# Turning the exponentials through DRAM and VectorE, and making the right sides' sums a batch earlier, in an attention and MLP kernel bound by TensorE

## The chip, the cores and the metric

One core of a Trainium2 chip runs the whole kernel. The metric is device microseconds of one execution. Each kernel below was executed several times; medians and ranges are given. A run whose granted TensorE clock fell far below 1 is called slow and is left out of every comparison.

## The reference, cut to what matters

```python
B, H, S, Ns, D = 8, 8, 512, 32, 64            # x: (B,H,S,D), state: (B,H,Ns,D)
a     = softmax(scale * x @ state.T)          # tokens read the state
xread = a @ state
a2    = softmax(scale * state @ x.T)          # the state reads the tokens
sread = a2 @ x
t     = concat(xread, sread) -> (B * 544, 512)
out   = gelu_quick(t @ w_in) @ w_out          # 512 -> 2048 -> 512, all in float32
```

A "batch" below is one of the 8 values of B: 512 tokens that pass through both matrices.

## The kernel before

The down product of a batch (2048 to 512) is made by Strassen's scheme with seven products P1 to P7 of blocks. Some of the seven are themselves made by a second level, again seven products of 128-column blocks: "two-level". While TensorE works on batch b, VectorE and ACT prepare batch b + 1 through hooks, which are called between the products by name: "P6.3" is after the third small product of P6. A small product is eight matmuls, and below it is called an "eight". T1 to T4 are sums of blocks of `w_out`, the right sides of P5, P6, P7 and P4; P3 has the block B22. In the hooks, `x_scale` and `x_back` are steps of the tokens' side of the attention (division, transposes back); `att_eT` and `eT_turn` belong to the state's side.

For sread, the exponentials of the scores `e` (state rows by tokens) must be turned so that tokens are rows. TensorE did it, between P6 and P3 of the batch before:

```python
def att_eT(b, g):
    ps = att_ps([P, SCH, P], f"eT_{b}_{g}")
    for c in range(SCH):
        nc.tensor.transpose(ps[:, c], a["e2"][g][0][:, P*c : P*(c+1)], ident)
    nc.scalar.copy(a["eT"][:, g], ps)
...
def s_norm(b, g):                              # e is divided by its sum, on ACT
    nc.scalar.activation(out=e, in_=e, func=AF.Copy, scale=sm)
```

Batch 1 was `plain`: only P6 and P7 of it were two-level, since the sums of the right sides (blocks of `w_out`) for the second level were only made on VectorE during batch 1:

```python
if plain:
    p5 = bank(0)
    product(p5, [S1[:, f, :half] for f in range(HF)], T1, "P5")
...
ahead = {   # VectorE's work for later batches, hung into batch 1
    "P1a": low_sums(T2, low_a) + [(low_keep, ...), (T_of, (T4, B21, T2)), (low_third, (T2,))],
    "P1b": low_sums(T3, low_b) + [(low_keep, ...), (low_third, (T3,))],
    "P4.7": low_sums(T1, low_b) + [...],
}
for k, step in zip((4, 5, 6), low_sums(B22, low_a)):
    ahead[f"P7.{k}"] = [step]
```

A set of sums (three 128x512 pieces, 768 KB) is kept in DRAM and reloaded before its product; there is SBUF room for two sets, and one more for T4's.

```python
def low_load(k, i):
    nc.sync.dma_start(turn_rooms[i], outside[k])
```

## Time and profile before

| | before |
|---|---|
| time, median (range) | 718.16 us (718.05 to 718.18, 4 runs) |
| span of the profiled run | 716.2 us |
| TensorE busy / VectorE busy | 703.9 us (98%) / 586.9 us (82%) |
| start of the next batch's scores to the same in the next batch, batches 2 to 6 | 76.43 us |
| the same in batch 1 | 79.19 us |

The last two rows are the useful clock of this kernel. In TensorE's timeline each batch has one row of scores (output `o`, input `xsq`), and the distance of these rows is the length of a batch. The prediction shows the lines of the profile. In a timeline the columns are start, duration, engine, line, instruction, tiles and shapes, how many were merged and, in brackets, how long the engine idled before and what ended that. Of the tiles, `eT` holds the turned exponentials, `sr` is the result of the state read (sread), and `M` is what the states give with `w_in`.

### The profile page before, as it was taken

The page shows a single profiled execution, that of the slowest core. Times are in us where ns is not written, and L with a number is a line of the kernel's source. Part 1 is how long each engine was busy: PE and PEld are TensorE (multiplying, and loading weights), DVE is VectorE, ACT ScalarE, POOL GpSimd, SP SyncE. Part 2 cuts the span into 40 slices and gives each one's busy share as a digit, 9 for nine tenths or more (in the row PEclk, how much of TensorE's full clock was granted, in tenths as well). Part 3 has the DMA queues.
Part 4 walks back from the last instruction along what each step waited for, and adds up shares of the span by engine and source line. Part 5 has one row for each costly group of instructions (what it writes and reads, how often), then busy time and mean ns, then how long its engine had stood idle before and what let it go on. Part 6 is the DMA issues. An engine that isn't in the chain of part 4 may idle for free.

```text
span 716.2 us, 12329 instructions
## 1 busy us (share of the span) xinstructions
PE 703.9 (98%) x4949; PEld 561.0 (78%) x4951; DVE 586.9 (82%) x1199; ACT 241.8 (34%) x467; POOL 0.8 (0%) x8
## 2 busy tenths in 40 slices
PE   8989999999999999999999999999999999999996
PEld 3433444457898799889998899879987998899995
DVE  6999899739968998789878997898779987888650
ACT  5686511024214331424233422442243324300210
POOL 0000000000000000000000000000000000000000
PEclk9999999999999999999999999999999999999999
DMA  8921246016145234405450444132431440022001
GB/s 228 364 83 58 97 148 130 24 59 152 56 166 73 47 117 162 78 1 118 138 144 3 83 168 125 28 74 94 174 62 29 133 148 30 1 70 108 17 1 29
DMA packets 104362, 68.43 MB, mean 96 GB/s; under 512 B 87665, under 2 KB 95345, under 8 KB 104305
## 3 DMA queue, kind: packets, MB, share of 16 engines
q1 hardware_dynamic: 104304, 67.65, 33.4%
q8 instruction: 39, 0.64, 0.4%
q14 instruction: 19, 0.15, 0.1%
HBM read 54.79 MB, written 12.85 MB: 94 GB/s over the span
## 4 chain that ended last, share of the span: by engine, by line
PE 90%; DVE 3%; DMA 2%; ACT 2%; issue 0%; SPq 0%; DVEq 0%; ACTq 0%
PE low L669 19%; PE o L1071 17%; PE o L720 14%; PE o L669 9%; PE o L518 7%; PE h L500 7%; PE upx L1071 6%; PE M L320 4%; PE o L561 2%; PE o L320 1%; PE sr L480 1%; PE warm L125 1%; PE upx_sr L1071 1%; DMA out_dram<-osb_sr 1%; PE eT L469 1%; DMA out_dram<-osb 1%
## 5 line engine op out<-in xcount | busy, mean ns | idle before, releaser
L1081 DVE TENSOR_TENSOR g<-o,g 128x512 f32<-128x512 f32 (+1 forms) x140 | 88.0, 650 | 51.5 <-PE o L1071 50.5
L720 PE MATMUL o<-w_out,g 128*128 128x256 f32 x480 | 107.9, 381 | 0.0
L720 PEld LDWEIGHTS o<-w_out,g 128*128 128x128 f32 x480 | 90.1, 190 | 18.4 <-issue 6.3
L1078 ACT ACTIVATE g<-g 128x512 f32<-128x512 f32 (+1 forms) x84 | 49.8, 600 | 100.8 <-DVE g L1081 100.8
L1071 PE MATMUL upx<-aT,M 128*128 128x256 f32 x192 | 49.3, 379 | 0.0
L1071 PE MATMUL o<-ta,M 128*128 128x256 f32 x192 | 49.3, 379 | 0.0
L1071 PE MATMUL o<-ta,ms 128*128 128x256 f32 x192 | 48.3, 379 | 0.0
L460 ACT COPY M<-M 128x512 f32<-128x512 f32 x64 | 33.2, 596 | 29.7 <-PE M L320 29.7
L1071 PEld LDWEIGHTS o<-ta,ms 128*128 128x128 f32 x192 | 36.5, 190 | 5.0
L1071 PEld LDWEIGHTS o<-ta,M 128*128 128x128 f32 x192 | 36.5, 190 | 5.0
L669 PE MATMUL low<-low,g 128*128 128x128 f32 x304 | 40.2, 275 | 0.0
L1071 PEld LDWEIGHTS upx<-aT,M 128*128 128x128 f32 x192 | 36.1, 190 | 4.7
L669 PEld LDWEIGHTS low<-low,g 128*128 128x128 f32 x304 | 37.0, 192 | 0.0
L669 PE MATMUL low<-sums,later 128*128 128x128 f32 x264 | 35.0, 276 | 0.1
L669 PEld LDWEIGHTS low<-sums,later 128*128 128x128 f32 x264 | 32.7, 192 | 0.7 <-DVE pu L674 0.3
L320 PE MATMUL M<-w_in,stT 64*32 64x512 f32 x512 | 32.7, 594 | 0.2 <-ACT eT L470 0.2
L541 DVE TENSOR_TENSOR later<-g,g 128x512 f32<-128x512 f32 (+1 forms) x32 | 20.8, 649 | 14.3 <-ACT g L503 14.3
L500 PE MATMUL h<-low,M 128*128 128x512 f32 x64 | 29.7, 600 | 1.5 <-DVE low L408 1.5
L500 PE MATMUL h<-aT,M 128*128 128x512 f32 x64 | 28.7, 599 | 1.4 <-ACT M L460 1.4
L518 PE MATMUL o<-w_out,g 128*128 128x512 f32 x64 | 28.7, 594 | 0.0
L669 PE MATMUL low<-w_out,g 128*128 128x128 f32 x216 | 28.5, 275 | 0.0
L518 PE MATMUL o<-w_out,sums 128*128 128x512 f32 x64 | 28.4, 594 | 0.0
(214 smaller groups left out, 1287.9 us busy)
## 6 DMA issues: line engine op xcount, KB each, us to landing
low<-low SPq DMA_DIRECT2D x34, 768.0 KB
later<-in_moe_w_out_dram SPq DMA_DIRECT2D x16, 512.0 KB
xn<-in_x_dram SPq DMA_DIRECT2D x28, 256.0 KB
w_out<-in_moe_w_in_dram SPq DMA_DIRECT2D x12, 512.0 KB
xsq<-in_x_dram SPq DMA_DIRECT2D x96, 64.0 KB
out_dram<-osb SPq DMA_DIRECT2D x18, 256.0 KB
out_dram<-later SPq DMA_DIRECT2D x14, 256.0 KB
later<-in_moe_w_in_dram SPq DMA_DIRECT2D x4, 512.0 KB
```

The source lines that it names most:

```text
L125: nc.tensor.matmul(ps, zeros[:, :P], zeros, start=True, stop=True)
L320: nc.tensor.matmul(ps[g][st], A[b]["stT"][rows, st], rhs(rows, j), start=True, stop=True)
L460: nc.scalar.copy(m[:, g], ps[g])
L500: nc.tensor.matmul(hps, lhs[i], rhs[i], start=(i == 0), stop=(i == n - 1))
L518: nc.tensor.matmul(ops, G[key, f // 2][:, f % 2, P * r : P * (r + 1)], w_out[:, f], start=(f == 0), stop=(f == NF - 1))
L541: nc.vector.tensor_tensor(out=s1, in0=a21, in1=a22, op=ALU.add)
L561: nc.tensor.matmul(ps[:, r], lhs[f][:, P * r : P * (r + 1)], rhs[:, f], start=(first and r == 0 and f == 0), stop=(f == HF - 1), skip_grou ...
L669: nc.tensor.matmul(ps, lhs[f], rhs[:, f], start=(first and f == 0), stop=(f == QF - 1), skip_group_check=True)
L720: nc.tensor.matmul(ps[:, r], lhs[f][:, P * r : P * (r + 1)], rhs[:, f], start=(r == 0 and f == 0), stop=(f == HF - 1), skip_group_check=True,)
L1071: nc.tensor.matmul(ps[:, k], lhs[i][:, o : o + P], rhs[i], start=(first and k == 0 and i == 0), stop=(i == n - 1), skip_group_check=True,)
L1078: nc.scalar.activation(out=dst, in_=src, func=AF.Gelu_apprx_sigmoid)
L1081: nc.vector.tensor_tensor(out=dst, in0=ps, in1=x, op=ALU.add)
```

## The change

Its intent: take work off the engine that is the bound. The turns leave TensorE: `e` goes to DRAM in runs of 128 B, comes back with its 32x32 blocks in the right places, and VectorE turns each block. The division by the sums moves behind the state read. A reload is cut into three, in the order in which its parts are read. VectorE's sums for P6, P5, P3 and P7 are made in a hole, a stretch in which VectorE idles, at the end of batch 0, so that P5, P3 and P4 of batch 1 become two-level too. The core of the diff:

```diff
+    def eT_out(b):
+        for j in range(NPR):
+            src = e2_room[b][Ns*j : Ns*(j+1), :NG].rearrange("n g (t a) -> n (g t) a", a=Ns)
+            nc.sync.dma_start(squares[:, :, j], src)
+    def eT_in(b):
+        v = squares.rearrange("n (k i) j a -> i n k (j a)", i=SCH)
+        for i in range(SCH):
+            nc.sync.dma_start(a["eT"][Ns*i : Ns*(i+1)].rearrange("n g c q -> n (g c) q"), v[i])
+    def eT_turn(b, g):
+        t = A[b]["eT"][:, g].rearrange("p c q -> p (c q)")
+        nc.vector.transpose(t, t)
...
     def low_load(k, i):
-        nc.sync.dma_start(turn_rooms[i], outside[k])
+        for n in (1, 0, 2):
+            nc.sync.dma_start(low[:, 3*i + n], outside[k][:, FC*n : FC*(n+1)])
...  (hooks of the next batch)
-            ("P6.4", x_scale, 0), ("P6", att_eT, 0), ("P6", att_eT, 1),
-            ("P3.3", x_scale, 1), ("P3.4", x_back, 0), ("P3.5", x_back, 1)
+            ("P6.6", x_scale, 1), ("P3.3", x_back, 0), ("P3.4", x_back, 1),
+            ("P3.5", eT_turn, 0), ("P3.6", eT_turn, 1), ("P5", eT_in),
...  (end of batch 0)
         if f == NF - 2:
             T_of(T1, B12, B11)
+            low_away(6, B22)
+            low_made(5, T1, 1)
...
             T_of(B12, B22, B12)
+            low_away(3, T3)
+            low_third(T3)
             turn_x(2)
+            low_made(2, T2, 0)
...  (batch 1: all `plain` branches are gone)
+    ahead = {"P1a": [(low_third, (B22,)), (T_of, (T4, B21, T2)), (low_third, (T2,))],
+             "P7.7": [(low_third, (T4,))]}
```

More of the change, by code (lines that the diff above doesn't have):

```diff
@@ L360, in att_s_max @@
             a["mx2"].append(mx)
+    e2_room = {}
     def att_s_exp(b, room=None):
@@ L364, in att_s_exp @@
         if room is None:
-            room = apool.tile([P, NPR, S], FP32, tag="xT", name=f"e2_{b}")
+            room = e2_room[b] = apool.tile([P, NPR, S], FP32, tag="xT", name=f"e2_{b}")
         a["e2"] = []
@@ L379, in s_norm @@
             nc.vector.tensor_scalar(e, e, sm, None, ALU.mult)
-        else:
-            nc.scalar.activation(out=e, in_=e, func=AF.Copy, scale=sm)
     def att_s_norm(b):
@@ L460, in att_M @@
             nc.scalar.copy(m[:, g], ps[g])
+    squares = dram.tile([Ns, NG * NB, NPR, Ns], FP32, name="squares")
+    def eT_out(b):
+        for j in range(NPR):
+            src = e2_room[b][Ns * j : Ns * (j + 1), :NG].rearrange("n g (t a) -> n (g t) a", a=Ns)
+            nc.sync.dma_start(squares[:, :, j], src)
+    def eT_in(b):
+        a = A[b]
+        a["eT"] = apool.tile([P, NG, SCH, P], FP32, tag="eT", name=f"eT_{b}")
+        v = squares.rearrange("n (k i) j a -> i n k (j a)", i=SCH)
+        for i in range(SCH):
+            nc.sync.dma_start(a["eT"][Ns * i : Ns * (i + 1)].rearrange("n g c q -> n (g c) q"), v[i])
+    def eT_turn(b, g):
+        t = A[b]["eT"][:, g].rearrange("p c q -> p (c q)")
+        nc.vector.transpose(t, t)
     def att_eT(b, g):
@@ L484, in att_sread @@
         sr = apool.tile([P, P], FP32, tag="sr", name=f"sr_{b}")
-        nc.scalar.copy(sr, ps.rearrange("p g d -> p (g d)"))
+        if b < 2:
+            nc.scalar.copy(sr, ps.rearrange("p g d -> p (g d)"))
+        else:
+            for g in range(NG):
+                nc.scalar.activation(out=sr[:, D * g : D * (g + 1)], in_=ps[:, g], func=AF.Copy, scale=a["e2"][g][1])
         A[b]["sr"] = sr
@@ L618, in low_load @@
     def low_load(k, i):
-        nc.sync.dma_start(turn_rooms[i], outside[k])
+        for n in (1, 0, 2):
+            nc.sync.dma_start(low[:, 3 * i + n], outside[k][:, FC * n : FC * (n + 1)])
     def low_keep(k, src):
@@ L635, in low4_make @@
         low_keep(4, t)
+        a["low4"] = t
     def low4_load(a):
@@ L699, in strassen_two @@
     def strassen_two(key, dst, hooks, a4):
-        plain = a4 is None
         B11, B21, B22 = w_out[:, :HF, :HN], w_out[:, HF:, :HN], w_out[:, HF:, HN:]
@@ L767, in strassen_two @@
         nc.scalar.copy(k1, bank(0))
-        if plain:
-            sums_of((S2, (q1, q2, q4)))
-        else:
-            *r, p5 = spare_M()
-            r = [v.rearrange("p (k h t) -> p k h t", k=2, h=2) for v in r]
-            p5 = p5.rearrange("p (r n) -> p r n", r=2)
-            sums_of((S1, r), (S2, (q1, q2, q4)))
-            third_of(S1)
+        *r, p5 = spare_M()
+        r = [v.rearrange("p (k h t) -> p k h t", k=2, h=2) for v in r]
+        p5 = p5.rearrange("p (r n) -> p r n", r=2)
+        sums_of((S1, r), (S2, (q1, q2, q4)))
+        third_of(S1)
         product(bank(1), A_of(0, 1), B21, "P2")
@@ L787, in strassen_two, with at @@
         o, h0, h1 = low_banks()
-        if plain:
-            for fn in first:
-                fn()
-            p5 = bank(0)
-            product(p5, [S1[:, f, :half] for f in range(HF)], T1, "P5")
-            banks = [h0, h1, o]
-        else:
-            def at(i):
-                for fn in first[i - 1 : i]:
-                    fn()
-                hook(f"P5.{i}")
-            b11, t3, b21, b22 = halves_of(T1)
-            strassen_low(left_of(S1, *r), (b11, t3, b21, b22, *low_b), [h0, h1, o], p5, at)
-            low_load(6, 1)
-            o, h0, h1 = low_banks()
-            banks = [h0, o, h1]
+        def at(i):
+            for fn in first[i - 1 : i]:
+                fn()
+            hook(f"P5.{i}")
+        b11, t3, b21, b22 = halves_of(T1)
+        strassen_low(left_of(S1, *r), (b11, t3, b21, b22, *low_b), [h0, h1, o], p5, at)
+        low_load(6, 1)
+        hook("P5")
+        o, h0, h1 = low_banks()
+        banks = [h0, o, h1]
         def sums(y, rooms):
@@ L842, in strassen_two @@
         steps4, left4 = sums(y_of(NU, half), (q1, q2, q4))
-        own6 = {}
-        if not plain:
-            steps12, left12 = sums(y_of(NU, 0), r)
-            own6 = {2: steps12[:1], 5: steps12[1:2]}
+        steps12, left12 = sums(y_of(NU, 0), r)
+        own6 = {2: steps12[:1], 5: steps12[1:2]}
         lowly("P6", left_of(S2, q1, q2, q4), T2, low_a, banks, k2, own6)
-        if not plain:
-            low_load(3, 0)
+        low_load(3, 0)
         tt(k2, k2, k1)
         tt(t01, p5, k2)
-        if plain:
+        hook("P6")
+        p3 = o01
+        o, h0, h1 = low_banks()
+        own3 = {1: steps12[2:3], 2: steps12[3:]}
+        if key + 1 == B:
+            own3.update({i + 3: steps3[i : i + 1] for i in range(4)})
+        lowly("P3", left12, B22, low_b, [h0, h1, o], p3, own3)
+        if key + 1 < B:
+            low_load(5, 1)
+        hook("run")
+        if key + 1 < B:
             for fn in steps3:
                 fn()
-            hook("P6")
-            p3 = bank(3)
-            product(p3, A_of(0, 1), B22, "P3")
-            o, h0, h1 = low_banks()
-            lowly("P7", left3, T3, low_b, [h0, h1, o], k3, {})
-        else:
-            hook("P6")
-            p3 = o01
-            o, h0, h1 = low_banks()
-            own3 = {1: steps12[2:3], 2: steps12[3:]}
-            if key + 1 == B:
-                own3.update({i + 3: steps3[i : i + 1] for i in range(4)})
-            lowly("P3", left12, B22, low_b, [h0, h1, o], p3, own3)
-            if key + 1 < B:
-                low_load(5, 1)
-            hook("run")
-            if key + 1 < B:
-                for fn in steps3:
-                    fn()
-            hook("T")
-            o, h0, h1 = low_banks()
-            lowly("P7", left3, T3, low_a, [o, h0, h1], k3, {k + 1: steps4[k : k + 1] for k in range(4)})
-            if key + 1 < B:
-                low_load(2, 0)
+        hook("T")
+        o, h0, h1 = low_banks()
+        lowly("P7", left3, T3, low_a, [o, h0, h1], k3, {k + 1: steps4[k : k + 1] for k in range(4)})
+        if key + 1 < B:
+            low_load(2, 0)
         osb = opool.tile([P, 2, HN], FP32, tag="osb", name=f"osb_{key}_11")
@@ L887, in strassen_two @@
         ]
-        if not plain:
-            o, h0, h1 = low_banks()
-            lowly(
-                "P4", left4, T4, low_parts(a4["low4"]), [o, h1, h0], k1, {2: then[:2], 3: then[2:3], 4: then[3:]}
-            )
-            p4 = k1
-        else:
-            for fn in then:
-                fn()
-            product(bank(2), A_of(1, 1), T4, "P4")
-            for i in range(1, 8):
-                hook(f"P4.{i}")
-            p4 = bank(2)
+        o, h0, h1 = low_banks()
+        lowly(
+            "P4", left4, T4, low_parts(a4["low4"]), [o, h1, h0], k1, {2: then[:2], 3: then[2:3], 4: then[3:]}
+        )
+        p4 = k1
         tt(o10, p4, k3)
@@ L920, in hooks_next @@
         at("P2a", att_s_exp, b)
+        at("P2a", eT_out, b)
         at("P2a", x_max, b, 0)
         at("P2a", x_sub, b, 0)
-        if b > 2:
-            at("P5.1", x_exp, b, 0)
-            at("P5.6", att_s_norm, b)
-            at("P5.6", x_max, b, 1)
-            at("P5.7", x_sub, b, 1)
-            at("P6.1", x_exp, b, 1)
-        else:
-            at("P2a", x_max, b, 1)
-            at("P2a", x_sub, b, 1)
-            at("P2a", x_exp, b)
-            at("P2", att_s_norm, b)
+        at("P5.1", x_exp, b, 0)
+        at("P5.6", att_s_norm, b)
+        at("P5.6", x_max, b, 1)
+        at("P5.7", x_sub, b, 1)
+        at("P6.1", x_exp, b, 1)
         steps = up_sums(b)
@@ L937, in hooks_next @@
         attention = [
-            ("P6.1", x_sum, 0), ("P6.3", x_sum, 1), ("P6.3", x_inverse), ("P6.4", x_scale, 0), ("P6", att_eT, 0), ("P6", att_eT, 1),
+            ("P6.1", x_sum, 0), ("P6.3", x_sum, 1), ("P6.3", x_inverse), ("P6.4", x_scale, 0),
         ]
-        if b > 2:
-            attention += [("P3.3", x_scale, 1), ("P3.4", x_back, 0), ("P3.5", x_back, 1)]
-            names = {"T": range(5), "P7.5": (5, 6), "P7.6": (7,), "P4.1": (8,), "P4.5": (12, 13)}
-            run, turned = "run", "P7.2"
-        else:
-            attention += [("P6.5", x_scale, 1), ("P6.6", x_back, 0), ("P6", x_back, 1)]
-            names = {"P3a": range(7), "P7.1": (7,), "P7.2": (8,), "P7.3": (12, 13)}
-            run, turned = "P3a", "P3b"
-        attention += [(run, att_sread), (run, att_M, 3, True), (run, att_M, 2)]
+        attention += [
+            ("P6.6", x_scale, 1), ("P3.3", x_back, 0), ("P3.4", x_back, 1), ("P3.5", eT_turn, 0), ("P3.6", eT_turn, 1),
+            ("P5", eT_in), ("run", att_sread), ("run", att_M, 3, True), ("run", att_M, 2),
+        ]
+        names = {"T": range(5), "P7.5": (5, 6), "P7.6": (7,), "P4.1": (8,), "P4.5": (12, 13)}
         for name, fn, *args in attention:
@@ L953, in hooks_next @@
                 at(name, steps[i][0], *steps[i][1])
-        at(turned, att_srT, b)
+        at("P7.2", att_srT, b)
         return h
@@ L1223, in T_of, with low_made, low_away @@
         nc.vector.tensor_tensor(out=t, in0=x0, in1=x1, op=ALU.subtract)
+    def low_made(k, t, i):
+        for fn, args in low_sums(t, (low_a, low_b)[i]):
+            fn(*args)
+        low_keep(k, turn_rooms[i])
+    def low_away(k, t):
+        room = apool.tile([P, NPR, S], FP32, tag="xT", name=f"away_{k}").rearrange("p j t -> p (j t)")[:, : 3 * FC]
+        for fn, args in low_sums(t, low_parts(room)):
+            fn(*args)
+        low_keep(k, room)
     rest = list(range(2 * nper, NF))
@@ L1250 @@
             T_of(T2, B22, T1)
+            low_third(T1)
         if f == NF - 1:
@@ L1264 @@
             ahead = {"P1a": [(up_strassen(b, S, *parts_x(b), A[b]["sums"]), ())]}
-            if b == 2:
-                ahead["P3.6"] = [(low_third, (T4,))]
-        else:
-            ahead = {
-                "P1a": low_sums(T2, low_a)
-                + [(low_keep, (2, turn_rooms[0])), (T_of, (T4, B21, T2)), (low_third, (T2,))],
-                "P1b": low_sums(T3, low_b) + [(low_keep, (3, turn_rooms[1])), (low_third, (T3,))],
-                "P4.7": low_sums(T1, low_b) + [(low_keep, (5, turn_rooms[1])), (low_third, (T1,)), (low_third, (B22,))],
-            }
-            for k, step in zip((4, 5, 6), low_sums(B22, low_a)):
-                ahead[f"P7.{k}"] = [step]
-            ahead["P7.6"] += [(low_keep, (6, turn_rooms[0])), (low_load, (2, 0))]
+        else:
+            ahead = {"P1a": [(low_third, (B22,)), (T_of, (T4, B21, T2)), (low_third, (T2,))], "P7.7": [(low_third, (T4,))]}
         if b + 1 < B:
@@ L1293 @@
         a4 = {}
-        at = hooks.setdefault("run" if b > 1 else "P3a", [])
+        at = hooks.setdefault("run", [])
         k = 3 if b + 1 < B else 0
         at[k:k] = [(low4_load if b > 1 else low4_make, (a4,))]
-        strassen_two(b, out_of(b), hooks, a4 if b > 1 else None)
+        strassen_two(b, out_of(b), hooks, a4)
         if b + 2 < B:
```

## The prediction

> **What bounds the kernel now.** I read the busy shares first, then the chain that ended last, then one table of windows by stage, and then the timelines of TensorE and VectorE inside two batches. From the page, the busy shares and the chain's share by engine:
>
> ```profile
> PE 703.9 (98%) x4949; PEld 561.0 (78%) x4951; DVE 586.9 (82%) x1199; ACT 241.8 (34%) x467; POOL 0.8 (0%) x8
> ...
> PE 90%; DVE 3%; DMA 2%; ACT 2%; issue 0%; SPq 0%; DVEq 0%; ACTq 0%
> ```
>
> TensorE is busy for 98% and carries 90% of the chain. The ends of matmuls are modelled, so I check with starts. In the windows (length, then PE, PEld, DVE and ACT busy with counts), batch 1 is the first row and two later batches follow:
>
> ```profile
> 154.30:233.50 79.20, 78.89 (x539) 67.22 (x538) 61.69 (x112) 25.56 (x47) 0.00 (x0) 1.00 0.43 111
> 233.50:310.00 76.50, 76.50 (x612) 68.08 (x611) 66.40 (x140) 27.26 (x54) 0.00 (x0) 1.00 0.35 94
> 310.00:386.50 76.50, 76.50 (x612) 68.08 (x611) 65.80 (x139) 27.26 (x54) 0.00 (x0) 1.00 0.36 95
> ```
>
> From batch 2 on TensorE never stops. The scores of the next batch start at 244.53, 320.96, 397.39, 473.82 and 550.25 us in the chain: a period of 76.43 us each time, so a later batch is worth exactly its TensorE instructions. Batch 1 runs from 165.27 to 244.53, 79.26 us, which is 2.83 more. Part of that is its three plain products, part is waiting. VectorE has about 10 us free in 76.5, but not evenly. Around P3 of the batch at 386 us (start, duration, instruction, in brackets the idle time before it):
>
> ```profile
> 416.37 0.29 DVE L674 TENSOR_TENSOR later<-o,pu 128x128 f32<-128x128 f32 x1 [0.48 <-PE o L669]
> ...
> 419.10 0.29 DVE L674 TENSOR_TENSOR pu<-low,pu 128x128 f32<-128x128 f32 x1 [0.24 <-PE low L669]
> ...
> 420.81 0.29 DVE L674 TENSOR_TENSOR later<-o,pu 128x128 f32<-128x128 f32 x1 [0.16 <-PE o L669]
> ...
> 423.49 0.29 DVE L674 TENSOR_TENSOR later<-low,pu 128x128 f32<-128x128 f32 x1 [0.60 <-PE low L669]
> ```
>
> There are 1.48 us of slack in these 7 us; from 391 to 415 us it has hardly any.
>
> **What the Trainium skill says.** "VectorE: DVE Perf Modes", section "The three transpose paths": TensorE turns a whole 128x128 into PSUM, VectorE only 32x32 blocks. That is why the new route needs a trip through DRAM to place the blocks besides VectorE's turn. The trace has the sizes for fp32: TensorE 8 instructions (two 128x512 turns) in 0.89 us, VectorE 0.68 us for each 128x512. "DMA: Bandwidth & Descriptors", section "Specifications": below 512 B a transfer is not at line rate. The new trip writes runs of 32 floats, 128 B. The trace agrees on the kind: the squares of x, also 128 B runs, 1 MB, take about 10 us (440.7 to 452 in the DMA row, 105 to 145 GB/s), while the 768 KB reloads reach 415 GB/s. Its section "Two DMAs through the same engine are not ordered": a DMA that reads what another wrote must wait for the completion semaphore; here that is a wait on the queue's issuing engine, which holds back what stands behind it. The kernel before has such pairs (sums kept in DRAM and reloaded), but tens of microseconds apart, so its trace doesn't time this wait.
>
> **The change part by part.**
>
> 1. Transposes of the exponentials off TensorE. Timeline of TensorE, the two-level product before, the transposes and the product after:
>
> ```profile
> 415.27 1.06 PE L669 MATMUL o<-low,later 128*128 128x128 f32 x8
> 416.17 1.04 PE L469 MATMUL eT<-ident,e 128*128 128x128 f32 x8
> 417.04 1.06 PE L669 MATMUL low<-w_out,g 128*128 128x128 f32 x8
> ```
>
> From 416.17 to 417.04 is 0.87 us; the general spacing of such eights is 0.893 (417.04 to 417.93). Six batches are prepared this way (2 to 7): 6 x 0.89 = 5.4 us of TensorE. ACT loses two copies of 0.59 and two scalings of 0.71 us per batch and gains one small instruction; it has room. VectorE gains two transposes, 2 x 0.6 to 0.7 = 1.3 us a batch.
>
> Do they fit? I walk VectorE through P6 and P3 of the batch at 386 us, with the spacing of the trace: 0.60 for a 128x512, 0.67 for two 128x256, 0.20 for an addition from PSUM, which can begin 0.2 to 0.27 after its eight matmuls were issued; TensorE goes on 0.33 after that addition began. P3 now begins at 416.15. The scaling moved to P6.6 uses the 0.48 slack. Then the additions of P3 fall at 418.80, 420.30, 421.12, 421.95 and 422.75, with the two backward transposes and the two turns between them. TensorE wants to begin its sixth and seventh eight at 420.61 and 421.51 and can at 420.63 and 421.45. The second turn ends at 422.85, and the second half of the state read would begin at 422.9. It just fits; P7 then finds its additions 0.2 late, which it can hide. So I take the whole 0.89 in a batch: five later batches give 4.5 us. Perhaps 0.1 to 0.3 of each is lost, since the margins are 0.05.
>
> The trip: exponentials end at 404.0. Four DMAs of 1024 runs, 512 KB at the 105 GB/s of the squares: 5 us, plus some 2 us, so landed at 411 to 412. The way back has 512 B runs, some 3 to 4 us (an estimate), landed at 416. The turn wants it at 421.3. 5 us to spare.
>
> 2. Reloads in three parts. Same bytes, and the first third can be issued when its part was read for the last time, 4 us earlier. No wait of TensorE names a reload before, so this gains nothing by itself; it pays for the queue's new load, because the last reload before P3 now stands behind the trip to DRAM (needed at 417, landed by about 413 by my count).
>
> 3. Sums at the end of batch 0. Two-level products instead of plain ones for P5, P3 and P4 of batch 1. The plain one is 32 instructions at 0.216 = 6.91 us, the two-level one 56 at 0.1117 = 6.25:
>
> ```profile
> 171.56 7.07 PE L720 MATMUL o<-sums,later 128*128 128x256 f32 x32
> ...
> 202.81 7.07 PE L720 MATMUL o<-sums,g 128*128 128x256 f32 x32
> ```
>
> Three times 0.66 = 2.0 us. VectorE's sums moved to batch 0 are 12 instructions and two thirds, some 9 us, against this hole:
>
> ```profile
> 145.91 2.48 DVE L156 STREAM_TRANSPOSE xsq<-xsq 128x512 f32<-128x512 f32 x4
> 159.92 0.69 DVE L541 TENSOR_TENSOR later<-g,g 128x512 f32<-128x512 f32 x1 [11.52 <-ACT g L503]
> ```
>
> The last three have to wait for the last up projection at 154.4 (they overwrite its right side) and end by 157. The hole takes all of it; the end of batch 0 does not move.
>
> But batch 1 has little VectorE room of its own. It starts at 159.92 as before, since that waits for ACT. Then 2.0 of sums, 3.7 for T4 and two thirds, 4.2 for the sums of P5 and P6: 169.6. From there a later batch needs 5.3 to its first addition of P5: 174.9, where P5, begun at 171.35, wants it at 173.4. ACT's exponentials are late with it and hold the first copy of P5. Walking on: 0.95 us of TensorE waits in P5, 0.15 in P6, 0.1 in P3. After the state read T4's own sums (2.06 us) stand on VectorE ahead of the sums of P7: its second eight waits 0.9, its fifth 0.9, its sixth 0.6. All waits: 3.6 us, where batch 1 now has about 0.86 (2.83 less 1.97). So batch 1 gets 2.0 + 0.9 - (3.6 - 0.86) = 0.1 us. This is the softest number here: ops placed one slot otherwise move it by 1 us either way.
>
> Sum: 4.5 + 0.1 = 4.6 us, 713.5. I lean a little to the better side for batch 1, because a wait that overlaps another counts twice in a walk by hand: 713.3.
>
> **The rivals.** (a) TensorE stays the bound everywhere and all its savings arrive: 5.4 + 2.0 + some of the old waits = 7.4 to 8.2 us, 710 to 711. For it: 98% busy, periods equal to 0.01 us. Against it: the walk of batch 1. (b) VectorE becomes the bound around P3 in every batch: the turns are 1.3 us in a stretch with 1.48 of slack that also gets 0.89 shorter. If its instructions cost 10% more than I walked, each batch loses 0.5: 716. (c) The trip through DRAM is late: writes of 128 B at half the rate of such reads would land at 416, the reload behind them after 417, and the turn at 421 to 422. It would cost 1 to 2 us in each of six batches: 716 to 722, the gain gone. Against it are 4 to 5 us of margin at the rate of the trace. (d) The reloads and the bytes to DRAM hurt elsewhere: DMA share is 0.36 in a batch at most, so no.
>
> **Range and chances.** Between (a) at 710.5 and a mild (b) or (c) at 716.2 lies what I would expect 8 times in 10, 713.3 in the middle. 2% would be 14.4 us, and all of TensorE's savings are about 8; a loss of 2% would need 2.4 us more in each of six batches over what is saved. Faster by over 2%: 0.01; within 2%: 0.98; slower: 0.01.
>
> **What the profile after should show.** No transposes of exponentials after batch 1; the period of later batches 75.5 to 75.8, TensorE idle there below 0.3; batch 1 between 77.5 and 80 with waits of TensorE on VectorE in P5 and P7; VectorE's hole before 159.9 nearly filled; the turns in P3 not waiting for DMA, and TensorE's state read waiting for them under 0.3. I would be wrong if the later period stays at 76.4 (rival b or c, the wait named there tells which), or if batch 1 shows 76 (my walk too dark) or over 81.

## The result, and the profile after

The changed kernel took 713.85 us (713.74 to 714.17, 4 runs), before 718.16: 4.31 us less. The ratio is 0.9941 with a 95% interval of 0.9924 to 0.9958. Ratios are the mean time of one kernel's fast runs over that of the other's of the same rounds, so not quite the ratio of the medians.

From the page of the changed kernel, the busy shares and the chain by engine:

```profile
PE 697.9 (98%) x4973; PEld 557.9 (78%) x4975; DVE 602.0 (85%) x1246; ACT 231.2 (32%) x456; POOL 0.8 (0%) x8
...
PE 93%; ACT 2%; DVE 2%; DMA 2%; SPq 0%; issue 0%; DVEq 0%; ACTq 0%
```

TensorE lost 6.0 us of busy time, but the span lost only 4.2; VectorE gained 15. So some 2 us of TensorE's savings came back as waits. The windows say where (the same two stretches as in the prediction):

```profile
154.30:233.50 79.20, 77.26 (x604) 67.82 (x603) 66.90 (x140) 25.11 (x51) 0.00 (x0) 1.00 0.50 134
233.50:310.00 76.50, 76.50 (x608) 68.08 (x607) 67.28 (x142) 25.86 (x52) 0.00 (x0) 1.00 0.46 109
```

In the second stretch TensorE still never idles. In the first, batch 1, it idles 1.94 us where it idled 0.31 before. (A pipelined matmul that starts late with its predecessor still draining does not count as idle, so the starts show a little more.) The distances of the scores are 78.91 us for batch 1 and 75.62 or 75.63 for each later batch, so the gain is 0.28 in batch 1 and 0.81 in each later one.

What a later batch looks like now, in TensorE's timeline: the last two eights of P3 and the state read behind them, and then the weight loads (PEld) of P3's fifth and sixth eight.

```profile
418.73 1.12 PE L696 MATMUL o<-w_out,spare_M 128*128 128x128 f32 x8
419.69 1.06 PE L696 MATMUL low<-low,g 128*128 128x128 f32 x8
420.68 1.10 PE L500 MATMUL sr<-xn,eT 128*32 128x64 f32 x64
```

```profile
417.73 0.97 PEld L696 LDWEIGHTS low<-w_out,g 128*128 128x128 f32 x8
418.69 0.97 PEld L696 LDWEIGHTS o<-w_out,spare_M 128*128 128x128 f32 x8
```

An eight takes 0.893 us when nothing holds it. The last one starts 0.96 after its predecessor: a wait of 0.07. It arises one eight earlier: the first weight load of the sixth eight comes 0.96 after that of the fifth. That eight writes the PSUM tile `o` that the fourth wrote, and VectorE's addition that reads it starts at 418.39 only, behind a turn of 128x512. The state read starts 0.99 after that, and it started 0.98 after it in the kernel before too, so it doesn't wait for the new turns.

Batch 1, TensorE's timeline in P5 (first line) and P7 (the others), the only eights with a wait of more than 0.2:

```profile
176.76 1.16 PE L696 MATMUL o<-sums,spare_M 128*128 128x128 f32 x8 [0.27 <-DVE spare_M L701]
...
195.78 1.13 PE L696 MATMUL low<-low,later 128*128 128x128 f32 x8 [0.35 <-ACT M L460]
...
199.75 1.16 PE L696 MATMUL low<-w_out,g 128*128 128x128 f32 x8 [0.94 <-DVE pu L701]
201.28 1.16 PE L696 MATMUL low<-w_out,later 128*128 128x128 f32 x8 [0.38 <-DVE later L701]
```

By starts, P5 takes 7.10 us (171.55 to 178.65) and P7 8.90 (194.27 to 203.17), where seven eights and, in P7, one small transpose take 6.25 and 6.36. What VectorE does meanwhile, around the state read:

```profile
192.53 0.69 DVE L1210 TENSOR_TENSOR low<-sums 128x512 f32<-128x512 f32 x1 [0.77 <-PE sr L500]
...
194.59 0.75 DVE L752 TENSOR_TENSOR later<-g,g 128x256 f32<-128x256 f32 x2
```

The first row is the first of T4's three sums, and the other two follow it. They wait for the state read, because their room is the one that holds x, and only then come the sums that P7 itself needs. The wait that the profile puts down to ACT (195.78) is most likely of the same kind: the second eight of P7 needs the sums which VectorE finishes by half at 195.69. And the hole of VectorE at the end of batch 0 has been filled as planned:

```profile
154.89 1.42 DVE L1210 TENSOR_TENSOR low<-sums,low 128x512 f32<-128x512 f32 x2 [0.17 <-PE h L524]
159.93 0.69 DVE L565 TENSOR_TENSOR later<-g,g 128x512 f32<-128x512 f32 x1 [3.62 <-ACT g L527]
```

Of 11.52 us, 3.62 are left, and batch 1's own work on VectorE begins at 159.93 as before.

### The profile page after: what moved, and what is told of

It is laid out like the page before. It is cut to its first block, busy times and chain, and to the rows that moved or that the text cites. A ratio compares the mean times of both kernels' runs of the same rounds, so it can differ in the third digit from the quotient of the medians.

```text
span 712.0 us, 12663 instructions
## 1 busy us (share of the span) xinstructions
PE 697.9 (98%) x4973; PEld 557.9 (78%) x4975; DVE 602.0 (85%) x1246; ACT 231.2 (32%) x456; POOL 0.8 (0%) x8
## 4 chain that ended last, share of the span: by engine, by line
PE 93%; ACT 2%; DVE 2%; DMA 2%; SPq 0%; issue 0%; DVEq 0%; ACTq 0%
PE low L696 21%; PE o L1058 17%; PE o L745 14%; PE o L696 10%; PE o L542 8%; PE h L524 7%; PE upx L1058 6%; PE M L320 4%; PE o L585 2%; PE o L320 1%; PE sr L500 1%; PE warm L125 1%; PE upx_sr L1058 1%; DMA out_dram<-osb_sr 1%; DMA xn<-in_x_dram 1%; DVE g L752 1%
## 5 line engine op out<-in xcount | busy, mean ns | idle before, releaser
L745 PE MATMUL o<-w_out,g 128*128 128x256 f32 x448 | 100.5, 380 | 0.0
L745 PEld LDWEIGHTS o<-w_out,g 128*128 128x128 f32 x448 | 84.2, 190 | 16.9 <-issue 5.5
L696 PE MATMUL low<-low,g 128*128 128x128 f32 x336 | 44.4, 275 | 0.0
L696 PEld LDWEIGHTS low<-low,g 128*128 128x128 f32 x336 | 40.9, 192 | 0.0
L696 PE MATMUL low<-sums,later 128*128 128x128 f32 x280 | 37.1, 275 | 0.0
L696 PEld LDWEIGHTS low<-sums,later 128*128 128x128 f32 x280 | 34.6, 192 | 0.5 <-ACT pu L705 0.2
L696 PEld LDWEIGHTS low<-w_out,g 128*128 128x128 f32 x224 | 27.3, 192 | 1.1 <-DVE pu L701 1.1
```

The lines of the kernel that those rows point to most:

```text
L696: nc.tensor.matmul(ps, lhs[f], rhs[:, f], start=(first and f == 0), stop=(f == QF - 1), skip_group_check=True)
L745: nc.tensor.matmul(ps[:, r], lhs[f][:, P * r : P * (r + 1)], rhs[:, f], start=(r == 0 and f == 0), stop=(f == HF - 1), skip_group_check=True,)
```

## The experiments

All ten runs gave the reference's result. The time of the kernel before was 718.12 to 718.16 us (medians of 7 to 9 runs) beside them.

Theory: the later batches gain because TensorE is their only bound and VectorE's new work just fits (0.81 each); batch 1 gains nothing to speak of, since the 2.0 us of its products come back as waits on VectorE, in P5 because VectorE starts late, in P7 because T4's sums stand in front. Rivals: the gain comes from the sums or the products; VectorE or the trip through DRAM bounds the later batches; batch 1's waits have one common cause.

### Each part alone

**turn_only** is the kernel before with the new route for batches 3 to 7 and the reloads in three parts; batch 1, and the preparation of batch 2 in it, are as before.

```diff
 (before, hooks for b > 2)
-    ("P6", att_eT, 0), ("P6", att_eT, 1), ("P3.3", x_scale, 1), ("P3.4", x_back, 0), ("P3.5", x_back, 1)
+    ("P6.6", x_scale, 1), ("P3.3", x_back, 0), ("P3.4", x_back, 1),
+    ("P3.5", eT_turn, 0), ("P3.6", eT_turn, 1), ("P5", eT_in)
```

> The kernel before with part 1 in batches 3 to 7 alone (batch 2 prepared by TensorE, batch 1 with its three plain products, sums as before), reloads in three parts. Theory: each of the five later periods loses the transposes less 0.06, 0.81 us as in the changed kernel: 5 x 0.81 = 4.1 us, so 714.1, with the later period at 75.62 and batch 1 unchanged at 79.26. Rival (the sums at the end of batch 0 and the three products carry the gain, or free VectorE for the turns): 716 or more, the period over 75.9.

Measured: 714.60 us, ratio 0.995 (0.9937 to 0.9964). One of its five executions took 912 us at a clock of 0.754, and that was the profiled one, so its trace is of no use. It gained 0.5 us less than expected, so the same kernel ran again for a fast trace:

> The same kernel as turn_only, whose profile fell in a run at a clock of 0.75. It gained 3.56 us where 4.05 were expected. Theory: the later periods are 75.62 as in the changed kernel, and 0.5 us is lost at one place in batch 1 or 2, where the trace of a fast run will show a wait. Rival: each of the five later periods is 75.7 to 75.75.

Measured: 714.54 us (714.48 to 714.60). The periods are 79.19 for batch 1, 76.00 for batch 2, and 75.63 for each later one. So 0.37 of the missing 0.5 is in batch 2. VectorE's and TensorE's timelines there:

```profile
269.20 0.67 DVE L1252 TENSOR_TENSOR sums<-sums 128x512 f32<-128x512 f32 x1
269.79 0.70 DVE L481 STREAM_TRANSPOSE eT<-eT 128x512 f32<-128x512 f32 x1
```

```profile
269.73 0.65 PE L501 MATMUL sr<-xn,eT 128*32 128x64 f32 x32
270.55 0.65 PE L501 MATMUL sr<-xn,eT 128*32 128x64 f32 x32 [0.16 <-DVE eT L481]
```

The old kernel has one more instruction here in this batch alone, the third of T4 in P3.6 (269.20), and it stands before the second turn. The second half of the state read waits for that turn. 0.6 us more of VectorE cost 0.37 us of time: the first sign that VectorE's slack at this place is used up. The theory stands: each period gains 0.80, and the loss is at one place.

**sums_only** is the reverse: the changed kernel with TensorE's turns and ACT's scaling put back.

```diff
 (changed)
-    at("P2a", eT_out, b)
-    ("P6.6", x_scale, 1), ... ("P3.5", eT_turn, 0), ("P3.6", eT_turn, 1), ("P5", eT_in)
+    ("P6", att_eT, 0), ("P6", att_eT, 1), ("P3.3", x_scale, 1), ("P3.4", x_back, 0), ("P3.5", x_back, 1)
```

> The changed kernel with part 1 undone: exponentials turned by TensorE and scaled by ACT as before, the five two-level products in batch 1 and the sums at the end of batch 0 kept. Theory: the products save 2.0 us, but TensorE's waits on VectorE in P5 and P7 of batch 1 cost 2.6 us more than the old ones (3.5 against 0.86): 0.3 to 0.8 us slower than before, 718.4 to 719.0, batch 1 at 79.6 to 80.1. Rival (all of TensorE's savings arrive): 716.2, batch 1 at 77.3 or less.

Measured: 718.91 us (718.77 to 719.10), 0.75 more than before; the ratio is 1.0011 (0.9998 to 1.0023, so 1 is just inside, though the ranges of the times don't meet), batch 1 takes 79.72, each later batch 76.43 or 76.44. TensorE's timeline shows the same waits in P7 to 0.01 us:

```profile
200.68 1.16 PE L698 MATMUL low<-w_out,g 128*128 128x128 f32 x8 [0.94 <-DVE pu L703]
202.22 1.16 PE L698 MATMUL low<-w_out,later 128*128 128x128 f32 x8 [0.38 <-DVE later L703]
```

So the two-level products of batch 1, as they stand, don't pay. Three products save 3 x 0.66 us of TensorE and lose slightly more to waits. The whole gain of the change is part 1: 0.81 in each of batches 2 to 6, and in batch 1 the 0.81 of its own turns less the 0.53 that sums_only lost there, 4.3 us together.

### Where batch 1's waits come from

**up_first** gives VectorE an earlier start. In ACT's timeline the last gelu of batch 0 (159.29) stood behind four copies, three of which waited for the DMA that empties the one output buffer (2.13 to 2.18 us each).

```diff
     for f in range(NF):
+        if f == NF - 1:
+            up_x(1, rest.pop(0))
         for r in range(SCH):
             down(0, r, [f], out_x[0, r], r == SCH - 1)
...
-        if f % 2 == 1:
+        if f % 2 == 1 and f < NF - 1:
             up_x(1, rest.pop(0))
```

> The changed kernel, batch 0's last up projection put before the last down products, so that its gelu on ACT does not stand behind the four copies that wait for output DMAs. Theory: VectorE's last sums of batch 0 begin at 156.3 in place of 159.9, and the 0.9 us of TensorE waits in P5 of batch 1 go; the waits in P7 stay: 713.0. Rival (P5 waits for ACT's exponentials or for sums, however early they begin): 713.7 to 713.9.

Measured: 713.21 us (713.11 to 713.61), ratio 0.9933 (0.992 to 0.9945), batch 1 at 78.08. VectorE's timeline, and TensorE's in P5:

```profile
155.46 0.69 DVE L565 TENSOR_TENSOR later<-g,g 128x512 f32<-128x512 f32 x1
```

```profile
175.20 1.06 PE L696 MATMUL low<-sums,later 128*128 128x128 f32 x8
176.10 1.06 PE L696 MATMUL o<-sums,spare_M 128*128 128x128 f32 x8
```

VectorE begins at 155.46 without a wait, and the eights of P5 follow each other at 0.89. P5's wait is gone, P7's is still there (0.94 and 0.38 again). The expectation was 713.0.

**t4_late** takes T4's sums out of the way, into P7.5 to P7.7, and shifts VectorE's work for the next batch behind them.

```diff
-    def low4_make(a): ... low_sums(T4, ...) at once, behind the state read
+    at("P7.5"), at("P7.6"), at("P7.7"): one of the three sums of T4 each, then low_keep(4)
-    names = {"T": range(5), "P7.5": (5, 6), "P7.6": (7,), "P4.1": (8,), "P4.5": (12, 13)}
+    names = {"T": range(5), "P4.1": (5, 6), "P4.5": (7,), "P4.6": (8,), "P4.7": (12, 13)}   # b == 2
```

> The changed kernel, T4's three sums of batch 1 moved from behind the state read to P7.5 to P7.7, and the next batch's sums after them into P4. Theory: the 2.06 us on VectorE ahead of P7's own sums cause P7's waits (2.54 us over its 6.36): P7 falls to 6.4 to 6.8 us, P4 gets up to 0.4 of waits: 711.7 to 712.2. Rival (P7 is late because the state read and the products M end late, or VectorE is behind since P5): gain under 0.5, 713.4 or more.

Measured: 711.47 us (711.43 to 711.50), ratio 0.9907 (0.9892 to 0.9922), batch 1 at 76.49. TensorE's timeline from the start of P7 to that of P4:

```profile
194.41 1.16 PE L699 MATMUL o<-w_out,g 128*128 128x128 f32 x8
195.41 1.06 PE L699 MATMUL low<-low,later 128*128 128x128 f32 x8
...
199.09 1.06 PE L699 MATMUL low<-w_out,later 128*128 128x128 f32 x8
...
200.87 1.06 PE L699 MATMUL o<-sums,g 128*128 128x128 f32 x8
```

P7 takes 6.46 us in place of 8.90, and the second eight waits 0.1 in place of 0.6 though ACT's copies are where they were. That wait too belonged to VectorE, not to ACT. P4 has no waits either, so the time is a little better than I expected. The edit moved the next batch's sums too, but in the changed kernel these began at 202.02, behind P7's last wait, so they were not its cause. The order of 2 us of VectorE's work was worth 2.4 us.

**both** has the two edits together.

> The changed kernel with both earlier moves: last up projection of batch 0 first, T4's sums in P7. Theory: the two causes of batch 1's waits are separate (P5: late start of VectorE; P7: T4's sums), so the gains add: 713.85 less 0.64 less 2.38 = 710.8, batch 1 at 75.7. Rival (one wait hides the other): 711.4, batch 1 at 76.4.

Measured: 710.54 us (710.48 to 710.85), ratio to before 0.9895 (0.988 to 0.9911), batch 1 at 75.63 and so equal to the later ones. The gains add: 0.64 and 2.38 make 3.02, and 3.31 was measured. The waits had two causes. This version is faster than both kernels, by 7.6 us than the one before, and TensorE is the only bound in batch 1 as in the later ones. Its windows (the first stretch had 1.94 us of idle in the changed kernel):

```profile
154.30:233.50 79.20, 79.20 (x619) 70.28 (x618) 68.68 (x142) 25.73 (x52) 0.00 (x0) 1.00 0.51 135
```

### The reloads in three parts

**whole_reload** is the changed kernel with each reload in one DMA.

```diff
-        for n in (1, 0, 2):
-            nc.sync.dma_start(low[:, 3*i + n], outside[k][:, FC*n : FC*(n+1)])
+        nc.sync.dma_start(turn_rooms[i], outside[k])
```

> The changed kernel with each reload in one DMA again. Theory from its trace: before P3 the reload is issued at 257.0 in batch 2 and P3's second eight wants it at 263.9; a whole one took 4.6 us to land (median), so it lands at about 262 and nothing changes: 713.7 to 714.3. Rival (the thirds pay for the trip's load on the queue): P3's second eight waits 0.5 to 2 us in each of six batches, 717 to 726.

Measured: 714.75 us (714.28 to 715.00), 0.9 more than the changed kernel and outside what I expected, but not by the rival's amount. Later periods are 75.62 or 75.63, unchanged. Batch 1 takes 79.33, 0.42 more, and TensorE's timeline in P3 has the reason:

```profile
185.26 1.06 PE L694 MATMUL low<-w_out,g 128*128 128x128 f32 x8
186.53 1.13 PE L694 MATMUL low<-low,spare_M 128*128 128x128 f32 x8 [0.21 <-DMA low<-low]
```

The second eight starts 1.27 after the first, 0.38 late, and waits for the reload. It is issued at 179.15 there and in the changed kernel in thirds from 177.44. So the thirds are needed, but only in batch 1. Another 0.27 us lies before batch 1 (its scores begin at 165.53; in the other fast runs at 165.23 to 165.38). No reload is at work there, and I leave that part open. What remains of the 0.9 is within the spread of the runs.

### How much room the new route has

**trip_twice** writes the exponentials to DRAM twice, first to a spare place.

```diff
+            nc.sync.dma_start(spare_squares[:, :, j], src)
             nc.sync.dma_start(squares[:, :, j], src)
```

> The changed kernel, the trip's 512 KB written to DRAM twice (first to a spare place). Theory from the trace (trip landed about 3.5 us before the turn, the reload about 2 us before P3's second eight): the queue needs 3.1 us more to issue and the engines about 4 us more, so P3 waits 1 to 3 us for reload or turn in each of six batches: 719 to 730. Rival (5 us of margin as predicted): 714 to 715.

Measured: 719.25 us (718.63 to 722.11), ratio 1.0023 (1.0007 to 1.0039). The periods are 79.44, 77.42, 75.98, 75.69 and 76.65: uneven, from 0.06 to 1.8 us over the undisturbed. TensorE's weight loads waited for turns that waited for the trip (first: waits in total, times, longest; then VectorE's timeline in batch 2):

```profile
PEld sr L503 <- DVE eT L483: 4.0, 9, 1.2
...
270.75 0.71 DVE L483 STREAM_TRANSPOSE eT<-eT 128x512 f32<-128x512 f32 x1 [1.75 <-DMA eT<-squares]
```

In five of the six batches the first turn waited for the trip, 0.20 to 1.75 us. So the trip has room, but less than one more write takes. The traffic of the changed kernel's trip itself (KB per DMA, median us from issue to landing; the trace tells the landing of only 4 of the 24 in each line):

```profile
squares<-e SPq DMA_DIRECT2D x24, 128.0 KB, 3.1
eT<-squares SPq DMA_DIRECT2D x24, 128.0 KB, 5.1
```

In batch 2 the four reads back are issued from 257.64 to 260.2; with 5.1 us to land, the last is there at about 264.6 (an estimate from the median), and the first turn starts 17.64 us after the start of P5, at 268.1: some 3.5 us of room. In batch 1 the trace tells when the last one landed: 3.0 us after its issue at 182.67, 4.3 us before the first turn at 190.04.

**turn_thrice** makes each turn three times, which gives the same result.

```diff
-        nc.vector.transpose(t, t)
+        for _ in range(3):
+            nc.vector.transpose(t, t)
```

> The changed kernel, each of VectorE's turns made three times (the result is the same): 2.5 us more of VectorE in P3 of each batch. Theory (VectorE's slack ahead of the state read is used up to 0.1 us): the state read waits 2.3 to 2.5 us in each of six batches, nothing is made up later: 727.5 to 729. Rival (there is slack, or VectorE makes it up in P7 and P4): 714 to 718.

Measured: 731.43 us (730.36 to 732.42), ratio 1.0185 (1.0171 to 1.0199); the last three periods are 78.37 or 78.38, 2.75 over the changed kernel's. Three turns took 2.19 us where one takes 0.69, so VectorE had 3.0 us more per batch, not the 2.5 that I expected, and TensorE waited for nearly all of it. But two batches lost more: batch 1 takes 82.11 (3.20 over the changed kernel's) and batch 2 80.01 (4.38 over). Batch 2 in TensorE's timeline and in windows of 2 us (the column of 1.00 or 0.54 is the granted clock):

```profile
273.52 0.65 PE L501 MATMUL sr<-xn,eT 128*32 128x64 f32 x32 [0.85 <-DVE eT L481]
275.81 0.80 PE L501 MATMUL sr<-xn,eT 128*32 128x64 f32 x32 [1.63 <-DVE eT L481]
276.53 3.43 PE L320 MATMUL M<-w_in,stT 64*32 64x512 f32 x32
```

```profile
276.00:278.00 2.00, 2.00 (x48) 0.81 (x47) 2.00 (x7) 0.52 (x2) 0.00 (x0) 0.54 0.21 37
278.00:280.00 2.00, 2.00 (x25) 0.34 (x10) 1.97 (x7) 1.07 (x2) 0.00 (x0) 0.60 0.83 320
```

After the two waits the 32 products `M` took 3.43 us where they take 1.95: the clock was granted at one half for some 3.4 us (0.46 and 0.40 of 2 us, each doubled), and the stretches before and after show 1.00. Batch 1 has the same from 194.3, within its second wait. The Trainium skill describes this: "TensorE: Matmul & The Clock Gate", section "What's actually happening", has a monitor of activity halve the clock after an idle window of about 3.4 us. Here it came with waits of at most 1.63 us. All six batches have the same two waits (0.84 or 0.85 and 1.63), and four of them kept the full clock, so the waits alone don't decide it. That the page's mechanism is at work is my reading; the halved clock and its length are measured. The profiled run is one of the two slower ones (732.3 us, mean clock 0.995); the other two took 730.4 to 730.5 at 0.997 and have no trace.

**both_swap** tests what is left of P3's wait: the turns come before the backward transposes.

```diff
-    ("P3.3", x_back, 0), ("P3.4", x_back, 1), ("P3.5", eT_turn, 0), ("P3.6", eT_turn, 1)
+    ("P3.3", eT_turn, 0), ("P3.4", eT_turn, 1), ("P3.5", x_back, 0), ("P3.6", x_back, 1)
```

> The kernel with both moves, and in P3 the turns ahead of the backward transposes (P3.3 and P3.4), so that the state read waits for nothing of VectorE. Theory: the last 0.06 to 0.1 us of waits before the state read go in each of six batches, if the trip has landed 1.3 us earlier than it is needed now (3.5 us of margin): 710.0 to 710.4, period 75.54 to 75.58. Rival (the margin of the trip is less than 1.3 us): 711 or more.

Measured: 710.75 us (710.65 to 711.12), periods of 75.63 or 75.64 like both's: neither gain nor loss. The trip landed in time even for turns 1.6 us earlier, so its room is at least that. And the wait did not go:

```profile
415.56 1.13 PE L699 MATMUL o<-w_out,spare_M 128*128 128x128 f32 x8
416.52 1.06 PE L699 MATMUL low<-low,g 128*128 128x128 f32 x8
```

The last eight of P3 again starts 0.96 after the sixth. This expectation was wrong about the cause. The state read never waited; what waits is the sixth eight, for the PSUM tile that the fourth wrote. The addition that reads it starts at 415.22, behind a 128x512 turn on VectorE, whichever turn that is.

## Why the prediction was right

The time, 713.85, is 0.55 above the predicted 713.3 and inside 710.5 to 716.2. By its own steps:

- **TensorE as the only bound of the later batches.** Right. turn_again, which has the new route alone, gains 3.6 of the 4.3 us in five batches, and sums_only shows no gain from the rest.
- **0.89 us in each.** A little large: 0.81 was measured, since 0.87 us of transposes were taken out and the sixth eight of P3 now waits 0.07. The walk had that eight late by 0.02. This term is the mis-sized one, 0.08 x 5 = 0.4 us, just under the loss of 0.1 to 0.3 a batch that the text allowed but didn't take into its sum.
- **VectorE's new work just fits.** Right, and turn_thrice shows how closely: of 3.0 us more, 2.75 arrive in the time. P3 began 1.89 earlier than in the walk (414.26), and VectorE's additions in it fell within 0.1 us of the walked places, shifted by that.
- **The trip in time.** Right, with 3.5 us of room (estimated) or 4.3 (batch 1) rather than 5. The doubled trip showed rival (c) to be real one write further on.
- **Reloads in three parts gain nothing by themselves.** Right for the later batches. That they pay for the queue's new load showed in batch 1 alone (0.4 us in whole_reload).
- **The hole at the end of batch 0.** Right: VectorE was through at 156.3 and went on at 159.93.
- **Batch 1: 2.0 + 0.9 less 2.7.** Right. The walk gave waits of 0.95 in P5 and 2.4 in P7; 0.85 and 2.54 were measured, and batch 1 gained 0.28 where 0.1 was foreseen. t4_late and up_first confirm the two causes as the walk named them. Three figures on the way are a little off: the printed addends from 159.92 make 169.8, not 169.6 (the 3.7 was 3.5 in the trace, and 169.6 and 174.9 were both met); 2.0 + 0.9 - 2.74 is 0.16; and 79.26 takes its two ends from two views, where one view gives 79.19.
- **The last step**, the lean from the sum of 713.5 to 713.3, was meant for batch 1 and rested on a reason that nothing had measured. Batch 1 did come out 0.18 better than the walk's 0.1; the later batches' 0.4 put the time on the other side of the sum.

## What to carry to other kernels

When one engine is busy for 98%, what is taken off it counts only where its next instruction doesn't wait for the engine that got the work: list that engine's instructions in program order through the tight stretch and add up, since here such a list gave each wait to 0.3 us. Sums that nobody needs at once should not stand in an engine's program ahead of sums that the bound engine waits for (moving them was worth 2.4 us, more than half of the whole change). And an order of instructions on ACT that looks harmless can set the start of VectorE: the gelu behind four copies cost 0.6 us two stages later.

## What the Trainium skill lacked or had wrong

- "TensorE: Matmul & The Clock Gate", sections "What's actually happening" and "HAM oscillation — how this bites in real kernels": the rule is to have no idle gaps beyond some 3.4 us. In turn_thrice the clock was halved for about 3.4 us in two of six batches, from during or just after the second of two waits (0.84 or 0.85 and 1.63 us) with 32 narrow matmuls (0.65 us) between them. The page does say, in the section after these, that short idles between groups of matmuls can do it, but not how long they have to be.
- "VectorE: DVE Perf Modes", section "The three transpose paths": the figures are for bf16 128x128. In fp32, VectorE took 0.69 us for a 128x512 (0.75 each when one follows on the other's output), and TensorE's 128x128 turns followed each other at 0.11 us within a stream of matmuls.
- "DMA: Bandwidth & Descriptors", section "Specifications": it says that below 512 B a transfer is not at line rate, without a trn2 rate for writes from SBUF. Here 128 KB in runs of 128 B took 3.1 us from issue to landing (median of the 4 landings that the trace tells, 2.7 to 5.1; four DMAs were issued one after another). Each such issue held the queue's engine for 0.69 us (median of 24; 0.57 to 1.60).
- No page says how long TensorE needs to go on after the addition that frees its PSUM bank: in the walk, 0.33 us after the addition's start (0.05 after its end) held for the three waits of batch 1 that were checked (0.33 or 0.34).
